# Window attention into a SiLU MLP: another order of the work ahead of the MLP, and of the attention beside it

## The chip, the core and the metric

The kernel runs on one core of a Trainium2 chip. TensorE (PE in the profile; PEld is its weight loads), VectorE (DVE), ScalarE (ACT) and GpSimd (POOL) each work through their own instructions in order; SyncE (SP) issues most of the DMAs, in order too. The metric is the device time of one launch in microseconds; lower is better. The three timed runs lie within 0.24% of one another.

## The reference

```python
def _attn_ref(q, k, v):                       # (8, 8, 576, 64) each
    scores = scale * np.matmul(q, k.transpose(0, 1, 3, 2))
    bias = slopes[:, None, None] * (-np.abs(rel))[None, :, :]
    mask = (rel >= 0) & (rel < 128)
    scores = np.where(mask, scores + bias[None], -1000000000.0)
    scores = scores - np.max(scores, axis=-1, keepdims=True)
    attn = np.exp(scores)
    attn = attn / (np.sum(attn, axis=-1, keepdims=True) + 1e-09)
    return np.matmul(attn, v)
...
x = attn_out.transpose(0, 2, 1, 3).reshape(4608, 512)
h = x @ w_in                                  # 512 x 2048
g = h * (1.0 / (1.0 + np.exp(-h)))
return g @ w_out                              # 2048 x 512
```

A query looks at itself and the 127 positions before it. The attention's output, with the heads side by side, is the input of a SiLU MLP.

## The kernel before

**Attention in pairs.** The 4608 tokens are 36 tiles of 128. Two batches of 576 tokens make nine tiles, and tile `i` needs the keys and values of tiles `i - 1` and `i`. Its eight heads are done in two halves of four, so there are 72 "pairs" `p = 2i + q`. A pair goes through these steps: `scores` (16 matmuls into the PSUM tiles `sp`; 8 in the first tile of two batches), `row_max` (four DVE instructions that add the bias from `tab` and take the maximum), `exps` (four ACT instructions), `p_hi` and `p_lo` (ACT and DVE: the probabilities as an fp16 high and low part, tile `hr`, two buffers), `p_transpose` (two DMA transposes issued by SP, into `hl`), `attend` (24 matmuls into `av`, with V's two parts `v1`, `v2`), `normalize` (DVE: sum, reciprocal, product), and for tiles from the fifth on `x_hi` and `x_lo` (ACT and DVE). Tiles 0 to 3 leave their output as fp32 `x` instead, and `x_transpose` (PE, then ACT and DVE) makes the MLP's first input `xh`, `xl` of it, one chunk of 128 columns at a time. Later tiles go through a DMA transpose and `x_parts` (ACT and POOL).

**V's scale.** `v_hi` (POOL) and `v_lo` (DVE) need one power of two for each two batches of V. `vscale_load` brings V in nine pieces of 256 KB, `vscale_reduce` reduces each to one column (an ACT instruction), and `vscale_finish` makes the scale `vsc` of them in three stages on DVE and PE. For the first two batches no `attend` can run before it.

**The MLP in groups.** A group is four tiles, 512 tokens; there are nine. For each of 16 slices `f` of the inner width, `gemm1` (`h`, 12 matmuls in two halves), `act1` (tanh, ACT), `act2` (DVE), `act3` (`gh`, ACT), `act4` (`gl`, POOL) and `gemm2` (`o`, 12 matmuls in two halves). Both matrices are kept as a high and a low part in SBUF, made once from the fp64 weights: `w_load`, then `w_split1`, `w_hi` (ACT), `w_shift`, `w_low`, `w_sign` (DVE), `w_lo` (DVE for `wil`, POOL for `wol`). Four of the 32 halves are made ahead of the MLP (`W_EARLY`), 28 beside its first group. The raw halves have two buffers.

**What sets the order.** Nothing is scheduled by a tool: the engines run what the program records, in that order. The program counts points; a group's 64 half-slices are points 0 to 63 of it (1 point is about 6 matmuls of the MLP), and negative points precede the MLP. `put(point, fn, ...)` plans a step, and `begin()` records a point's steps ahead of that point's matmuls. `at(p)` is the point of `scores(p)`; the pair's other steps have fixed distances to it. `later(n, ...)` puts a step `n` points on, behind what is planned there already. A group's last slice is special: `gemm2` of slices 14 and 15 follow each other, with `x_parts` of the next group's tiles between the halves, and `store` sends the group's output (two `ot` on ACT, two on DVE, with two buffers for all).

**PSUM.** During the MLP, `scores` takes both buffers of the bank `a`, `attend` takes one, and both wait for DVE to have read what was in them.

Of the kernel before, what the change touches and what calls it, by code (L numbers as in the profile page):

```python
# [6 lines left out]
F32 = mybir.dt.float32  # L7
# [24 lines left out]
GT = TG // P  # L32
NF = DFF // P
NCC = DM // P
# [5 lines left out]
VCH = 9  # L40
# [5 lines left out]

SLICE = 4
STEP = 8
LEAD = 26
XD = GT  # L50
LAST = [f"{kind}{f}" for f in (NF - 1, NF - 2) for kind in ("wih", "wil", "woh", "wol")]
WD = (1, 1, 1, 2, 3)
W_EARLY = (-52, -40, -28, -14)


def at(p):

    return STEP * (p - 2 * GT) - LEAD


@with_exitstack
def tile_window_attention_then_silu_mlp(ctx, tc, qk, v, w_in, w_out, base8, out):
    nc = tc.nc

    const = ctx.enter_context(tc.tile_pool(name="const", bufs=1))
# [32 lines left out]
    bank = {"scores": [("w", "x"), ("y", "z")], "av": ["a"], "misc": ["h"]}  # L98
    turn = {}
# [10 lines left out]
    vred = {}  # L110

    def vscale_load(b, i):
        tag, bufs = (LAST[4 + i % 4], 1) if b == 0 else ("rv", 2)
        t = pool.tile([P, DM], F32, tag=tag, bufs=bufs, name=f"vm{b}_{i}")
        (nc.scalar if b == 0 else nc.sync).dma_start(t, v[b, i * P : (i + 1) * P, :])
        vred.setdefault(b, {})[i] = t

    def vscale_reduce(b, i):
        t = vred[b][i]
        if i == 0:  # L120
            vred[b]["m"] = pool.tile([P, VCH], F32, tag="vm", name=f"vmx{b}")
        m = vred[b]["m"][:, i : i + 1]

        nc.scalar.activation(t, t, AF.Abs, accum_out=m)

    def vscale_finish(b, stage):
        r = vred[b]
# [138 lines left out]
    xt, whole, now = {}, [], [0]  # L266
# [40 lines left out]
    def x_transpose(cc):  # L307
        xp = ps_of(next_tag("misc"), f"xp{cc}")
        for i in range(GT):
            nc.tensor.transpose(xp[:, i * P : (i + 1) * P], xt[i][:, cc * P : (cc + 1) * P], ident)  # L310
        nc.scalar.copy(xh[:, cc], xp)  # L311
        nc.vector.tensor_sub(xl[:, cc], xp, f32(xh[:, cc]))  # L312
# [132 lines left out]
    def put(point, fn, *a):  # L445
        plan.setdefault(max(point, at(0)), []).append((fn, a))

    for p in range(NPAIR):
        i, q = divmod(p, 2)
        n = at(p)  # L450
        put(n, scores, p)
        if block_of(i) in (SPLIT, SPLIT + 1):
            put(n + 1, other_batch, p)
        put(n + 1, row_max, p, 0)
        put(n + 2, row_max, p, 1)
        put(n + 2, exps, p, 0)
# [12 lines left out]
        if q == 0:  # L469
            if i > 1:  # L470
                put(n - 14, load_q, i)
                put(n - 14, load_k, i)
            put(n - 2, load_v, i)
            put(n + 9, v_hi, i)
            put(n + 10, v_lo, i)
    for b in range(1, NBB):
        n = at(2 * NBLK * b)
        for i in range(VCH):
# [36 lines left out]
            fn(*a)  # L515

    with tc.manual_schedule():
        load_q(0)
        load_k(0)
        nc.scalar.dma_start(tab, base8)  # L520
        load_q(1)
        load_k(1)
        for i in range(4):
            vscale_load(0, i)
        make_identity(nc, ident)
        nc.gpsimd.memset(v1[:, :, :, D : D + 1], 1.0)
        nc.gpsimd.memset(ones, 1.0)
        for i in range(VCH):
            put(at(0) + 1 + i // 2, vscale_reduce, 0, i)
            if i + 4 < VCH:  # L530
                put(at(0) + 1 + i // 2, vscale_load, 0, i + 4)
        for x in range(3):
            put(at(0) + 6 + x, vscale_finish, 0, x)
        for n in range(2):
            put(at(0) + 4 + n, w_next_load)
        for n in W_EARLY:
            put(n, w_next)
        while pos[0] < 0:
            begin()
            pos[0] += 1  # L540
        bank.update(scores=[("a", "a")], misc=["a"])
        for cc in range(NCC - 1):
            turn["misc"] = -1
            bank["misc"] = ["h"]
            x_transpose(cc)
        bank["misc"] = ["a"]

        for g in range(NG):
            now[0] = g

            seq = []
            for f in range(NF):
                n = g * NF + f
                seq += [("g1", n, 0)] + [("xt", 0, NCC - 1)] * (n == 0) + [("g1", n, 1)]
                if 0 < f < NF - 1:
                    seq += [("g2", n - 1, 0), ("g2", n - 1, 1)]
            n = g * NF + NF - 1
            for i, x in enumerate([("g2", n - 1, 0), ("g2", n - 1, 1), ("g2", n, 0), ("g2", n, 1)]):
                if g + 1 < NG:
                    seq.append(("xt", g + 1, i))  # L560
                seq.append(x)
            for k, n, half in seq:
                if k == "xt":
                    if n == 0:
                        bank["misc"] = ["h"]
                        x_transpose(half)
                        bank["misc"] = ["a"]
# [58 lines left out]
```

## Time and profile before

| | |
|---|---|
| median of 3 runs | 1053.81 us (1052.30 to 1054.81) |
| the profiled execution | 1053.94 us, of which the span from the first to the last instruction is 1052.2 us |
| PE busy | 965.3 us, 92% of the span |
| DVE busy | 525.2 us, 50% |
| ACT busy | 464.8 us, 44% |
| POOL busy | 256.3 us, 24% |
| DMA | 109.62 MB, mean 104 GB/s |

Shares over the whole span hide that there are three stages: what precedes the MLP, the MLP's first group (with the weights made beside it), and the eight other groups. They are told apart by busy times in stretches of the span. Rows of the timeline give the start, the duration and, in brackets, the idle time of the engine just before with what ended it.

### The profile page before, as it was taken

Reading aid. Unit: us, or ns where it says so; the run is one execution under the profiler, and the core shown is the slowest. Engines: PE = TensorE matmul, PEld = TensorE weight load, DVE = VectorE, ACT = ScalarE, POOL = GpSimd, SP = SyncE. Lnnn points to the kernel's source line nnn. Section 1 sums busy time; section 2 is a strip of 40 time slices with the busy share of each in tenths; the row PEclk is TensorE's granted clock in tenths of the full one; section 3 lists DMA queues with packets and bytes.
Section 4 is the critical chain, followed back from the end, with each engine's and each line's share of the span. In section 5 each row is a group of like instructions: output and inputs, shape, how many; then the busy total and the mean of one; then the engine's idle time right before and its main releaser. Section 6 shows DMA issues by size and latency. Waiting matters only on the chain. (4 is left out here: it accounts for less than half of the span.)

```text
span 1052.2 us, 16631 instructions
## 1 busy us (share of the span) xinstructions
PE 965.3 (92%) x6204; PEld 773.6 (74%) x6204; DVE 525.2 (50%) x1374; ACT 464.8 (44%) x975; POOL 256.3 (24%) x236
## 2 busy tenths in 40 slices
PE   3557787799999999999999999999999999999998
PEld 2445666678887888788878887878788878887886
DVE  2777999944444544434445444434445444421111
ACT  5555656544445444534454445434534453423222
POOL 0011333332223222322232222222222232222221
PEclk9768999999999999999999999999999999999999
DMA  7885677644444444424454445423444443311001
GB/s 218 172 196 156 199 193 208 174 118 89 82 91 116 106 103 100 104 70 82 88 117 101 102 102 121 89 72 82 110 75 90 84 110 82 63 22 41 1 0 40
DMA packets 214560, 109.62 MB, mean 104 GB/s; under 512 B 181072, under 2 KB 189264, under 8 KB 214480
## 3 DMA queue, kind: packets, MB, share of 16 engines
q1 hardware_dynamic: 213040, 105.68, 43.1%
q10 hardware_dynamic: 1440, 2.88, 0.8%
q8 instruction: 49, 0.80, 0.3%
q14 instruction: 31, 0.25, 0.1%
HBM read 55.05 MB, written 9.44 MB: 61 GB/s over the span
## 5 line engine op out<-in xcount | busy, mean ns | idle before, releaser
L367 POOL TENSOR_TENSOR gl<-gt,gh 128x512 fp32r<-128x512 f32 x144 | 187.7, 1303 | 637.5 <-ACT gh L362 428.6
L351 ACT ACTIVATE gt<-h 128x512 f32<-128x512 f32 x144 | 85.6, 595 | 424.0 <-PE h L344 424.0
L344 PE MATMUL h<-xh,wih 128*128 128x512 f32 x576 | 237.6, 413 | 0.0
L379 PE MATMUL o<-woh,gl 128*128 128x512 f32 x576 | 226.0, 392 | 7.0 <-POOL gl L367 6.9
L344 PE MATMUL h<-xh,wil 128*128 128x512 f32 x576 | 226.4, 393 | 0.0
L344 PE MATMUL h<-xl,wih 128*128 128x512 f32 x576 | 226.0, 392 | 0.2 <-DVE xl L312 0.2
L379 PE MATMUL o<-woh,gh 128*128 128x512 f32 x576 | 225.4, 391 | 0.2 <-ACT gh L362 0.2
L379 PE MATMUL o<-wol,gh 128*128 128x512 f32 x576 | 224.3, 389 | 0.0
L356 DVE SCALAR_TENSOR_TENSOR gt<-gt,h 128x512 f32<-128x512 f32 x144 | 98.8, 686 | 249.2 <-ACT gt L351 249.1
L238 DVE SCALAR_TENSOR_TENSOR hr<-t,hr 128x512 f16<-128x512 f32 (+1 forms) x144 | 131.3, 912 | 91.8 <-ACT hr L233 91.1
L214 DVE CUSTOM_DVE_ANT_0 t<-sp,tab 128x256 f32<-128x256 f32 (+1 forms) x288 | 103.2, 403 | 80.3 <-PE sp L194 80.3
L379 PEld LDWEIGHTS o<-woh,gl 128*128 128x128 f32 x576 | 108.1, 188 | 36.6 <-POOL gl L367 14.3
L224 ACT ACTIVATE t<-t,mx 128x256 f32<-128x256 f32 (+1 forms) x288 | 121.2, 487 | 27.3 <-DVE mx L214 26.5
L344 PEld LDWEIGHTS h<-xh,wih 128*128 128x128 f32 x576 | 109.0, 189 | 25.7 <-ACT xh L311 0.4
L344 PEld LDWEIGHTS h<-xh,wil 128*128 128x128 f32 x576 | 108.8, 189 | 24.0
L379 PEld LDWEIGHTS o<-woh,gh 128*128 128x128 f32 x576 | 108.1, 188 | 22.8 <-ACT gh L362 0.5
L379 PEld LDWEIGHTS o<-wol,gh 128*128 128x128 f32 x576 | 108.1, 188 | 22.2
L344 PEld LDWEIGHTS h<-xl,wih 128*128 128x128 f32 x576 | 109.2, 190 | 19.9 <-DVE xl L312 0.5
L194 PE MATMUL sp<-k,q 64*128 64x128 f32 x1088 | 93.0, 309 | 23.0 <-DMA k<-qk 6.5
L194 PEld LDWEIGHTS sp<-k,q 64*128 64x128 f32 x1088 | 76.9, 207 | 46.8 <-issue 44.9
L362 ACT CAST gh<-gt 128x512 fp32r<-128x512 f32 x144 | 88.6, 615 | 33.3 <-DVE gt L356 33.3
L261 PEld LDWEIGHTS <-hl 128*128 128x128 f16 x1632 | 57.5, 101 | 51.6 <-issue 36.9
(52 smaller groups left out, 609.6 us busy)
## 6 DMA issues: line engine op xcount, KB each, us to landing
q<-qk SPq DMA_DIRECT2D x36, 256.0 KB, 3.5
k<-qk SPq DMA_DIRECT2D x36, 256.0 KB, 3.5
rv<-v SPq DMA_DIRECT2D x36, 256.0 KB, 3.0
out<-ot SPq DMA_DIRECT2D x36, 256.0 KB, 2.0
wr<-w_in SPq DMA_DIRECT2D x16, 512.0 KB, 4.0
wr<-w_out SPq DMA_DIRECT2D x16, 512.0 KB, 3.7
vm<-v SPq DMA_DIRECT2D x27, 256.0 KB, 3.2
vm<-v ACTq DMA_DIRECT2D x9, 256.0 KB, 3.6
```

The lines of the kernel that those rows point to most:

```text
L194: nc.tensor.matmul(sp[h][:, u, o], qs[i][rows, 2 * q + u], ks[i - 1 + o][rows, 2 * q + u], start=True, stop=True, skip_group_check=True,)
L214: nc.vector.tensor_tensor_reduce(out=t[:, h, 2 * P - n :], in0=st[p]["sp"][h][:, u, o].rearrange("p o c -> p (o c)"), in1=tab[:, 4 * q + 2 ...
L224: nc.scalar.activation(x, x, AF.Exp, bias=st[p]["mx"][:, 2 * u + h : 2 * u + h + 1], scale=-1.0)
L238: nc.vector.scalar_tensor_tensor(out=hr[:, 1], in0=t[:, :, 2 * P - n :], scalar=PSCALE, in1=hr[:, 0], op0=ALU.mult, op1=ALU.subtract)
L261: nc.tensor.matmul(av[:, 2 * u + h, : rhs.shape[-1]], lhs, rhs, start=(n == 0), stop=(n == len(seq) - 1), skip_group_check=True,)
L344: nc.tensor.matmul(hps[n], w[:, cc], x, start=(half == 0 and i == 0), stop=(half == 1 and i == len(seq) - 1), skip_group_check=True,)
L351: nc.scalar.activation(gt, hps[n], AF.Tanh, scale=0.5 / W_SCALE)
L356: nc.vector.scalar_tensor_tensor(out=gt, in0=gt, scalar=1.0, in1=hps[n], op0=ALU.add, op1=ALU.mult)
L362: nc.scalar.copy(gh, gt)
L367: nc.gpsimd.tensor_sub(gl, gt, f32(gh))
L379: nc.tensor.matmul(ops[ti], a[:, t], w, start=(f == 0 and i == 0), stop=(f == NF - 1 and i == len(seq) - 1), skip_group_check=True,)
```

## The change

It changes where steps stand. Pairs 0 to 7 keep a distance of 8 points; pairs 8 to 15 get points of their own (`CLOSE`, 6 apart), of which only pair 8 precedes the MLP; later pairs come 12 points later than before (`LEAD`). `attend` and what follows it get a distance of their own, `a`. The four early weight halves move behind pair 7's scores, and two of the four `x_transpose` now stand inside the first slice of the MLP. V's nine pieces get a buffer each (`LAST` grows from 8 tags to 16) and are loaded at once on SP's queue instead of four and five on ACT's; DVE reduces four of them. The bias table comes in two halves, and K and Q are loaded one tile earlier.

```diff
-LEAD = 26
+LEAD = 14
-LAST = [f"{kind}{f}" for f in (NF - 1, NF - 2) for kind in ("wih", "wil", "woh", "wol")]
+LAST = [f"{kind}{f}" for f in range(NF - 1, NF - 5, -1) for kind in ("wih", "wil", "woh", "wol")]
-W_EARLY = (-52, -40, -28, -14)
+CLOSE = (-4, 2, 8, 14, 20, 26, 32, 38)
+W_EARLY = (-18, -15, -12, -8)
 def at(p):
+    if p < 2 * GT:
+        return STEP * (p - 2 * GT) - 18
+    if p < 4 * GT:
+        return CLOSE[p - 2 * GT]
     return STEP * (p - 2 * GT) - LEAD
...
     def vscale_load(b, i):
-        tag, bufs = (LAST[4 + i % 4], 1) if b == 0 else ("rv", 2)
+        tag, bufs = (LAST[XD + i], 1) if b == 0 else ("rv", 2)
         t = pool.tile([P, DM], F32, tag=tag, bufs=bufs, name=f"vm{b}_{i}")
-        (nc.scalar if b == 0 else nc.sync).dma_start(t, v[b, i * P : (i + 1) * P, :])
+        nc.sync.dma_start(t, v[b, i * P : (i + 1) * P, :])
...
-        nc.scalar.activation(t, t, AF.Abs, accum_out=m)
+        if b == 0 and i % 2:
+            nc.vector.tensor_reduce(m, t, axis=AX.X, op=ALU.max, apply_absolute_value=True)
+        else:
+            nc.scalar.activation(t, t, AF.Abs, accum_out=m)
...
+        a = n + (20 if p < 2 * GT else 15 if p < 4 * GT else 13)
...
-        put(n + 20, attend, p)
-        put(n + 21, normalize, p, 0)
-        put(n + 22, normalize, p, 1)
-        put(n + 23, x_hi, p)
-        put(n + 24, x_lo, p)
+        put(a + 0, attend, p)
+        put(a + 1, normalize, p, 0)
+        put(a + 2, normalize, p, 1)
+        put(a + 3, x_hi, p)
+        put(a + 3, x_lo, p)
         if q == 0:
             if i > 1:
-                put(n - 14, load_q, i)
-                put(n - 14, load_k, i)
-            put(n - 2, load_v, i)
-            put(n + 9, v_hi, i)
-            put(n + 10, v_lo, i)
+                put(at(2 * i - 3) + 1, load_q, i)
+                put(at(2 * i - 3) + 1, load_k, i)
+                put(n - 2, load_v, i)
+            put(a - 3, v_hi, i)
+            put(a - 2, v_lo, i)
...
+        for cc, n in enumerate((23, 24)):
+            put(at(2 * GT - 2) + n, x_transpose, cc)
         while pos[0] < 0:
             begin()
             pos[0] += 1
         bank.update(scores=[("a", "a")], misc=["a"])
-        for cc in range(NCC - 1):
...
-            x_transpose(cc)
...
-                seq += [("g1", n, 0)] + [("xt", 0, NCC - 1)] * (n == 0) + [("g1", n, 1)]
+                seq += [("g1", n, 0)] + [("xt", 0, 2), ("xt", 0, 3)] * (n == 0) + [("g1", n, 1)]
```

How the engines' own orders change at the three places that matter below is shown in rows of the recorded program: line, operation, output<-inputs (a tile's name carries the pair, slice or piece it belongs to, then a buffer number), shape.

SP's queue at the start, before. `q`, `k`, `rv` are a tile's queries, keys and values, `wr` raw weights, `hl` a transposed probability tile; the nine pieces `vm0_*` and the table went through ACT's queue.

```order
L161 DMA q0_129<-qk 128x512
L157 DMA k0_131<-qk 128x512
L161 DMA q1_134<-qk 128x512
L157 DMA k1_136<-qk 128x512
L166 DMA rv0_159<-v 128x512
L246 DMA_TRANSPOSE hl0_0_193<-hr0_0_184 128x4x128
L398 DMA wr0_0_197<-w_in 128x4x256
```

And in the changed kernel, from the eighth of V's nine pieces on (`q0`, `k0`, half of the table and the pieces 0 to 6 stand ahead of these):

```order
L122 DMA vm0_7_147<-v 128x512
L122 DMA vm0_8_149<-v 128x512
L176 DMA rv0_151<-v 128x512
L171 DMA q1_153<-qk 128x512
L167 DMA k1_155<-qk 128x512
L542 DMA tab_65<-base8 128x8x128
L256 DMA_TRANSPOSE hl0_0_184<-hr0_0_176 128x4x128
```

All the loads of the start now share one queue, with `q1`, `k1` and the table's second half behind V's nine pieces.

DVE ahead of the MLP's first `act2`, before. The rows begin at the subtraction for the last transposed chunk of `x`; `wm2_0` is the fifth half of the weights, `hr11_0` belongs to pair 11, `gt0` is that `act2`.

```order
L312 TENSOR_TENSOR xl_126<-xp3_916,xh_125 128x512
L414 TENSOR_SCALAR wm2_0_914<-wm2_0_914 128x512
L419 SCALAR_TENSOR_TENSOR wm2_0_914<-wr2_0_635,wm2_0_914 128x512
L426 SCALAR_TENSOR_TENSOR wm2_0_914<-wr2_0_635,wm2_0_914 128x512
L238 SCALAR_TENSOR_TENSOR hr11_0_925<-t11_0_877,hr11_0_925 128x512
L356 SCALAR_TENSOR_TENSOR gt0_938<-gt0_938,h0_907 128x512
```

In the changed kernel, from pair 7's second `p_lo` on:

```order
L248 SCALAR_TENSOR_TENSOR hr7_1_596<-t7_1_561,hr7_1_596 128x512
L295 TENSOR_TENSOR x2_541<-av5_570,r5_600 128x256
L424 TENSOR_SCALAR wm0_0_607<-wm0_0_607 128x512
L429 SCALAR_TENSOR_TENSOR wm0_0_607<-wr0_0_242,wm0_0_607 128x512
L436 SCALAR_TENSOR_TENSOR wm0_0_607<-wr0_0_242,wm0_0_607 128x512
L186 SCALAR_TENSOR_TENSOR v2_68<-rv3_478,vsc0_226,v1_67 128x512
L450 TENSOR_TENSOR wil0_70<-wm0_0_607,wih0_69 128x512
L424 TENSOR_SCALAR wm0_1_617<-wm0_1_617 128x512
L429 SCALAR_TENSOR_TENSOR wm0_1_617<-wr0_1_295,wm0_1_617 128x512
L436 SCALAR_TENSOR_TENSOR wm0_1_617<-wr0_1_295,wm0_1_617 128x512
```

All five first halves of the weights (`wm0_0` to `wm2_0`) and pair 8 alone now stand between pair 7's last `p_lo` and the first `act2`; pairs 9, 10 and 11 are behind it.

ACT at the end of the third group (slice 47 is its last), before. `gt47` is tanh, `gh47` the high part that `gemm2` waits for; `xh` is `x_parts` of the next group, `vm2_8` a reduction for a later V scale, `x16` an `x_hi`.

```order
L351 ACTIVATE gt47_4371<-h47_4352 128x512
L331 ACTIVATE xh_125<-xt12_3457,vsc1_2047 128x4x128
L124 ACTIVATE vm2_8_4271,vmx2_3264<-vm2_8_4271 128x512
L331 ACTIVATE xh_125<-xt12_3457,vsc1_2047 128x4x128
L295 CAST x16_4387<-xs32_4375 128x256
L362 CAST gh47_4389<-gt47_4371 128x512
```

And in the changed kernel:

```order
L361 ACTIVATE gt47_4291<-h47_4271 128x512
L341 ACTIVATE xh_117<-xt12_3452,vsc1_2225 128x4x128
L234 ACTIVATE t33_0_4278<-t33_0_4278,mx33_4267 128x256 x2
L341 ACTIVATE xh_117<-xt12_3452,vsc1_2225 128x4x128
L234 ACTIVATE t33_1_4296<-t33_1_4296,mx33_4267 128x256 x2
L243 ACTIVATE hr33_0_4313<-t33_0_4278 128x512
L372 CAST gh47_4315<-gt47_4291 128x512
```

Pair 33's four `exps` and a `p_hi` now stand between the last slice's tanh and its `gh`. On PE, the scores that stood between `gemm2` of slices 14 and 15 (pair 35's, in this group) are replaced by pair 33's, one slice earlier, so that nothing stands between these two `gemm2`; and the group's last `attend` stands between the two halves of `gemm2` of slice 15 instead of behind the next group's first `gemm1`.

More of the change, by code (lines that the diff above doesn't have):

```diff
@@ L517, in tile_window_attention_then_silu_mlp @@
     with tc.manual_schedule():
+        make_identity(nc, ident)
+        nc.gpsimd.memset(ones, 1.0)
+        warm = const.tile([P, 1], F32, name="warm")
+        nc.scalar.activation(warm, ones[:, :1], AF.Exp)
         load_q(0)
         load_k(0)
-        nc.scalar.dma_start(tab, base8)
+        nc.sync.dma_start(tab[:, :, P:], base8[:, :, P:])
+        for i in range(VCH):
+            vscale_load(0, i)
+        load_v(0)
         load_q(1)
         load_k(1)
-        for i in range(4):
-            vscale_load(0, i)
-        make_identity(nc, ident)
+        nc.sync.dma_start(tab[:, :, :P], base8[:, :, :P])
         nc.gpsimd.memset(v1[:, :, :, D : D + 1], 1.0)
-        nc.gpsimd.memset(ones, 1.0)
         for i in range(VCH):
-            put(at(0) + 1 + i // 2, vscale_reduce, 0, i)
-            if i + 4 < VCH:
-                put(at(0) + 1 + i // 2, vscale_load, 0, i + 4)
+            put(at(0) + 3 + i // 2, vscale_reduce, 0, i)
         for x in range(3):
-            put(at(0) + 6 + x, vscale_finish, 0, x)
+            put(at(0) + 8 + x, vscale_finish, 0, x)
+        put(at(0) + 12, load_v, 1)
         for n in range(2):
-            put(at(0) + 4 + n, w_next_load)
+            put(at(0) + 14 + 8 * n, w_next_load)
         for n in W_EARLY:
             put(n, w_next)
+        for cc, n in enumerate((23, 24)):
+            put(at(2 * GT - 2) + n, x_transpose, cc)
         while pos[0] < 0:
@@ L564, in tile_window_attention_then_silu_mlp @@
                     if n == 0:
-                        bank["misc"] = ["h"]
                         x_transpose(half)
-                        bank["misc"] = ["a"]
                     else:
```

3 lines of the change are left out of this document (removed).

## The prediction

> **What bounds the kernel now.** First the busy times in the three stages. Columns: stretch, its length, busy us (instructions) of PE, PEld, DVE, ACT, POOL, granted clock, DMA share, GB/s.
>
> ```profile
> 0.00:94.10 94.10, 45.16 (x427) 37.26 (x428) 55.95 (x190) 50.77 (x113) 7.65 (x16) 0.76 0.76 188
> 94.10:209.40 115.30, 94.72 (x584) 73.58 (x584) 110.78 (x212) 68.20 (x139) 40.99 (x30) 1.00 0.70 191
> 209.40:226.60 17.20, 13.71 (x103) 10.77 (x103) 8.48 (x25) 8.84 (x21) 7.22 (x8) 1.00 0.52 128
> 226.60:1052.20 825.60, 811.70 (x5097) 652.01 (x5093) 350.00 (x950) 336.99 (x705) 200.48 (x182) 1.00 0.37 82
> ```
>
> In the last 826 us PE is busy for 812, so each wait added to PE there counts in full, and what DVE or ACT do counts only through such waits. In the MLP's first group DVE is busy for 96% of 115.3 us and PE for 82%: DVE is the bound. Ahead of it no engine reaches 60%: latency, a chain from step to step, is the bound. So the change can gain in the first stretch, can gain or lose DVE work in the second, and can only gain or lose waits in the last.
>
> Then the timeline of the first stretch (start, duration, engine, line, what; in brackets the wait before).
>
> ```profile
> 17.37 0.16 DVE L130 TENSOR_REDUCE vcol<-vmx 128x1 f32<-128x9 f32 x1 [1.89 <-ACT vm L124]
> 19.80 0.16 DVE L146 COPY vsc<-vs 128x2 f32<-128x2 f32 x1 [0.73 <-PE vs L144]
> 26.43 0.69 DVE L238 SCALAR_TENSOR_TENSOR hr<-t,hr 128x512 f16<-128x512 f32 x1 [1.47 <-ACT hr L233]
> 30.01 2.50 PE L194 MATMUL sp<-k,q 64*128 64x128 f32 x16 [2.39 <-DMA q<-qk]
> 32.76 0.69 DVE L238 SCALAR_TENSOR_TENSOR hr<-t,hr 128x512 f16<-128x512 f32 x1 [1.90 <-ACT hr L233]
> 37.49 0.69 DVE L238 SCALAR_TENSOR_TENSOR hr<-t,hr 128x512 f16<-128x512 f32 x1 [1.29 <-ACT hr L233]
> 59.23 0.69 DVE L238 SCALAR_TENSOR_TENSOR hr<-t,hr 128x512 f16<-128x512 f32 x1 [2.13 <-ACT hr L233]
> 94.09 0.68 DVE L356 SCALAR_TENSOR_TENSOR gt<-gt,h 128x512 f32<-128x512 f32 x1
> ```
>
> V's scale is ready at 20.0. The four L238 rows are the first `p_lo` of pairs 2, 3, 4 and 7; the last row is the first `act2`, with which the MLP's first group is in its stride. Pairs 2 to 7 come every 6.56 us on average ((59.23 - 26.43)/5), the fastest 4.73 after the one before.
>
> **The first stretch, term 1.** Up to the scale: 0 to 10 us moved 296 GB/s.
>
> ```profile
> 0.00:10.00 10.00, 1.22 (x8) 0.96 (x8) 0.93 (x8) 3.61 (x8) 0.95 (x8) 1.00 0.84 296
> ```
>
> Now the ninth piece is the 12th load of 0.262 MB: 3.15 MB, 10.6 us at that rate. Its reduction on ACT (0.8 us, an estimate from the 0.6 of ACT's other 128x512 rows, below) and the 2.6 us from `vcol` to `vsc` (17.37 to 19.96) give 14.0 us. `q1`, `k1` and the table's second half are loads 14 to 16, 4.19 MB, 14.2 us: next in line. From `vsc` to pair 2's first `p_lo` it took 6.5 us (19.96 to 26.43), which puts that at 20.6 (before 26.4). The four reductions on DVE have no row of their kind; they lie in DVE's idle time ahead of the scale (0.93 us busy in the first ten), so even at twice the 0.7 us of other 128x512 rows they cost nothing.
>
> Pairs 3 to 7: two things that slowed them leave this stretch, the waits for `q` (2.39 us in the row; K and Q now go out one tile earlier, behind transposes that are waited for anyway) and the early weight halves (2.5 us of DVE each, by the prices below). What stays is the loop `row_max`, `exps`, `p_hi`, `p_lo` over DVE and ACT and the two `hr` buffers, 4.73 at best, 6.56 as it was. I take 5.0, near the fastest, since what made it slower is gone: pair 7 at 45.6.
>
> From there to the first `act2` DVE has 44 instructions; their prices (mean ns after the bar):
>
> ```profile
> L214 DVE CUSTOM_DVE_ANT_0 t<-sp,tab 128x256 f32<-128x256 f32 (+1 forms) x48 | 16.8, 394 | 7.7 <-PE sp L194 7.7
> L238 DVE SCALAR_TENSOR_TENSOR hr<-t,hr 128x512 f16<-128x512 f32 (+1 forms) x23 | 14.7, 641 | 19.8 <-ACT hr L233 19.8
> L176 DVE SCALAR_TENSOR_TENSOR v<-rv,vsc,v 128x512 f16<-128x512 f32 x6 | 4.5, 746 | 1.2 <-POOL v L170 1.2
> L419 DVE SCALAR_TENSOR_TENSOR wm<-wr,wm 128x512 int32<-128x512 int32 x5 | 3.5, 691 | 0.2
> L312 DVE TENSOR_TENSOR xl<-xp,xh 128x512 fp32r<-128x512 f32 x4 | 2.7, 688 | 2.4 <-ACT xh L311 2.4
> L414 DVE TENSOR_SCALAR wm<-wm 128x512 int32<-128x512 int32 x5 | 2.4, 486 | 0.5 <-ACT wm L408 0.5
> L285 DVE TENSOR_TENSOR x<-av,r 128x256 f32<-128x256 f32 x8 | 3.3, 417 | 0.0
> L205 DVE MEMSET sp<- 64x384 f32 x4 | 1.5, 378 | 0.3 <-issue 0.2
> ```
>
> Five weight halves 5 x (0.49 + 2 x 0.69) = 9.3, two `wil` 1.4 and four `xl` 2.8 (0.69 each), four `p_lo` 2.6, pair 8's maxima 4 x 0.39 = 1.6, `v_lo` 0.7, two memsets 0.8, three `normalize` (0.42 and two short ones, some 0.8) 2.4: 21.6 us. Waits: before the first and third `xl` for PE's transposes and ACT (the L312 row: 2.4 in two), for a weight half that is loaded only when DVE has freed its buffer, for `p_lo`: 4.3 in all. So the first `act2` comes at 45.6 + 25.9 = 71.5 instead of 94.1: -22.6. Bounds: 4.73 and 6.56 a pair put it 1.4 lower or 7.8 higher.
>
> **The first group, term 2.** It is bound by DVE, so its DVE instructions count. To point 57, where the last weight half ends, it has one pair more: four maxima, two `p_lo`, a `v_lo` and (tiles 4 and 5 now lie here) two 64x384 memsets and four small ones: 1.6 + 1.3 + 0.7 + 1.4 = +5.0. These prices are those of the first stretch; in the group DVE is slower where POOL runs:
>
> ```profile
> L414 DVE TENSOR_SCALAR wm<-wm 128x512 int32<-128x512 int32 x27 | 17.4, 643 | 2.3 <-ACT wm L408 2.3
> L238 DVE SCALAR_TENSOR_TENSOR hr<-t,hr 128x512 f16<-128x512 f32 x14 | 16.1, 1152 | 0.0
> ```
>
> `p_lo` takes 1152 ns here against 641. POOL's 30 instructions there become 31, so I leave that toll as it is: 27 x 0.16 + 14 x 0.51 = 11.4 us on these two lines; half of it more or less is +-5.7.
>
> **Ends of groups, term 3.** Slice 15's `gh` decides. A slice of before with pair steps between tanh and `gh`, as now stands at each of the first seven groups' ends, and the third group's end:
>
> ```profile
> 634.12 0.39 PE L379 MATMUL o<-woh,gh 128*128 128x512 f32 x1
> 634.38 0.60 ACT L351 ACTIVATE gt<-h 128x512 f32<-128x512 f32 x1 [4.74 <-PE h L344]
> 634.88 1.70 ACT L224 ACTIVATE t<-t,mx 128x256 f32<-128x256 f32 x4
> 637.00 0.61 ACT L362 CAST gh<-gt 128x512 fp32r<-128x512 f32 x1
> 637.68 1.29 POOL L367 TENSOR_TENSOR gl<-gt,gh 128x512 fp32r<-128x512 f32 x1 [6.63 <-ACT gh L362]
> 641.16 0.71 ACT L331 ACTIVATE xh<-xt,vsc 128x512 fp32r<-128x512 f16 x1
> 643.22 1.16 PE L194 MATMUL sp<-k,q 64*128 64x128 f32 x16
> 644.31 0.50 PE L379 MATMUL o<-woh,gh 128*128 128x512 f32 x1
> 645.33 0.50 PE L379 MATMUL o<-woh,gl 128*128 128x512 f32 x1 [0.28 <-POOL gl L367]
> ```
>
> `gh` ended 3.49 us after `gemm2` of the slice before began (634.12 to 637.61). At a group's end two `xh` stand between as well, 0.62 each: 4.73, and `gl` 6.05. PE's cover is that `gemm2`, 2.72 us, without the scores of 1.09 (643.22 to 644.31) that followed it: 2.1 us of wait for `gh` and 0.8 for `gl`, 2.85 with the restart. Before, the third group's end lost 0.45 (645.33 for 644.88), the seven 1.6 together. 7 x 2.85 - 1.6 = +18.3. It can be less only if ACT's order let `gh` pass, which it can't; if `exps` were waited for, more.
>
> **Starts of groups, term 4.** There DVE sat behind an `ot` whose buffer was being stored, and with it a `row_max` that held the bank of the next `attend`, and `act2`. First PE's waits after the first group (us, times, longest), then three of them.
>
> ```profile
> PE av L261 <- DVE mx L214: 6.2, 7, 2.1
> PE o L379 <- POOL gl L367: 5.4, 11, 0.7
> 225.92 0.91 PE L261 MATMUL av<-v,hl 128*128 128x65 f16 x24 [2.08 <-DVE mx L214]
> 651.28 0.88 PE L261 MATMUL av<-v,hl 128*128 128x65 f16 x24 [0.67 <-DVE mx L214]
> 656.04 0.50 PE L379 MATMUL o<-woh,gl 128*128 128x512 f32 x1 [0.58 <-POOL gl L367]
> ```
>
> Now only a `normalize` (0.8 us) stands behind that `ot`, and the next scores come a whole `gemm1` later. By the spacing of the matmuls the waits of `av` cost 2.25 once and 0.83 six times, those of `gl` at starts of groups (six of the eleven) 0.74: -11.7. Late next is that `normalize`, with some 0.3 us to spare; 0 to -11.7 bounds it.
>
> **Clock, term 5, and moved work, term 6.**
>
> ```profile
> 223.20:226.60 3.40, 1.31 (x26) 0.96 (x25) 1.77 (x6) 0.70 (x3) 0.00 (x0) 1.00 0.42 157
> 226.60:230.00 3.40, 3.40 (x15) 2.72 (x12) 2.02 (x6) 1.70 (x4) 1.11 (x1) 0.50 0.20 40
> 124.20:127.60 3.40, 1.91 (x29) 1.75 (x30) 3.33 (x10) 3.03 (x7) 1.28 (x1) 1.00 0.68 220
> ```
>
> After 3.4 us with PE busy for 1.31 the granted clock was 0.50 for the next 3.4 us (15 matmuls in place of some 30: 1.7 us lost); after 1.91 it was not. That drop goes with its wait: -1.7. The new waits, 2.1 and 0.8 us within 3.4, leave as little as 0.5 busy; by where they fall on that grid the drop follows 61% (busy under 1.31) to 96% (under 1.91) of them. I take 75% at 1.6 us: 7 x 0.75 x 1.6 = +8.4; 0 and 11.9 bound it. The Trainium skill's page "TensorE: Matmul & The Clock Gate", section "Part 1: The HAM clock gate", has the clock fall after an idle window of about 3.4 us; by that rule these waits fill none, term 5 would be -1.7 and the sum -11.6. The rows above speak against it: 2.1 us idle sufficed.
>
> Two `scores` of 8 matmuls move from the first group to where PE is the bound: half of 1.09 each, +1.1.
>
> **Sum.** -22.6 + 5.0 + 18.3 - 11.7 + (8.4 - 1.7) + 1.1 = -3.2. Against the profiled execution's 1053.94 us (0.13 above the median) that is 1050.7.
>
> **Rivals.**
> - *The first pairs keep their pace* (the slower side): if transposes landing among loads, not the weights or `q`, held pairs 2 to 7, they stay at 6.56: +7.8, 1058.5. The brackets of the four `p_lo` rows name ACT's `hr`, which waits for just that buffer; against it the 4.73. It is slower than before by over 0.2% from 6.05 a pair on.
> - *The clock holds*: 1050.7 - 8.4 = 1042.3. For it, gaps of 2.4 us in the first group (the 1.91 row) that left the clock at 1.00. The Trainium skill's rule above would give this time too.
> - *No wait at the groups' ends*: without terms 3 and the new drops 1050.7 - 26.7 = 1024.0; only if ACT's rows ran otherwise than they stand.
> - *The first group takes back the front*: POOL's toll on DVE up by half, +5.7: 1056.4.
>
> **Numbers.** Forecast 52% (own range 1046 to 1056: 33 of it faster, 19 the same), first pairs 19% (2 the same), clock 16%, no waits 5%, first group 8% (half the same, half slower). Within 0.2% (2.1 us) is about what a measurement of this kernel cannot tell from no change. Faster 0.54, same 0.25, slower 0.21. The range leaves out 1024.0 and the tails of the others: 1041 to 1059.
>
> **What would show it.** First `act2` near 71 us; pairs 2 to 7 5 us apart; the first group's DVE busy over 95% and some 120 us from `act2` to slice 13; at each of seven group ends a PE wait for `gh` of 2 us and one for `gl` under 1, with clock 0.50 behind most; no waits of `av` at group starts. Wrong it is if the pairs' spacing or the waits at the ends are off: together they are 40 us against a sum of 3.

## The result: 1071.6 us, 1.8% slower, and the profile after

The changed kernel took 1071.64 us (median; 1071.01 to 1072.83) against 1053.69 of the kernel before on the same chip, a ratio of 1.0176 (95% interval 1.0163 to 1.0188). The forecast was 1050.7, at the outside 1059.0. The profiled execution has a span of 1069.2 us, 17.0 more than the 1052.2 of before. Every line number is 10 higher than before, from L124 on.

The stages, cut at the same points of the program as before:

```profile
0.00:75.88 75.88, 34.43 (x339) 28.81 (x341) 47.76 (x153) 38.74 (x85) 7.54 (x14) 0.78 0.78 200
75.88:199.86 123.98, 102.43 (x646) 81.05 (x644) 117.00 (x229) 75.11 (x152) 44.73 (x31) 0.92 0.67 183
199.86:217.10 17.24, 14.86 (x89) 11.19 (x88) 9.29 (x28) 8.63 (x16) 7.20 (x8) 0.90 0.80 187
217.10:1069.20 852.10, 832.75 (x5138) 658.80 (x5136) 404.30 (x970) 342.34 (x716) 204.53 (x183) 0.99 0.35 80
```

The first stretch is 18.2 us shorter, the first group 8.7 longer (123.98 for 115.30), and the last stretch 26.5 longer, of which 21.0 is PE's *busy* time (832.75 for 811.70, with 41 matmuls more). Of these 21.0 some 10 are six drops of the clock, in which a matmul takes longer (a term of the prediction), and some 1 is the moved `scores`; the rest, about 10 us, is what no step of the prediction had. The front, from the timeline of the changed kernel:

```profile
13.76 0.16 DVE L140 TENSOR_REDUCE vcol<-vmx 128x1 f32<-128x9 f32 x1 [0.75 <-ACT vm L134]
16.19 0.16 DVE L156 COPY vsc<-vs 128x2 f32<-128x2 f32 x1 [0.32 <-PE vs L154]
21.53 0.69 DVE L248 SCALAR_TENSOR_TENSOR hr<-t,hr 128x512 f16<-128x512 f32 x1 [1.21 <-ACT hr L243]
27.73 0.69 DVE L248 SCALAR_TENSOR_TENSOR hr<-t,hr 128x512 f16<-128x512 f32 x1 [2.44 <-ACT hr L243]
...
49.22 0.69 DVE L248 SCALAR_TENSOR_TENSOR hr<-t,hr 128x512 f16<-128x512 f32 x1 [1.26 <-ACT hr L243]
...
75.88 0.69 DVE L366 SCALAR_TENSOR_TENSOR gt<-gt,h 128x512 f32<-128x512 f32 x1 [0.23 <-ACT gt L361]
```

The scale is ready at 16.35, pair 2's first `p_lo` comes at 21.53, pair 7's at 49.22, 5.54 us apart on average, and the first `act2` at 75.88. Next PE's waits from 205 to 1000 us (us, times, longest), and the clock at the fourth group's end:

```profile
PE o L389 <- ACT gh L372: 13.0, 7, 1.9
PE o L389 <- POOL gl L377: 4.6, 9, 0.6
```

```profile
535.90:539.30 3.40, 1.05 (x4) 0.30 (x2) 0.71 (x2) 3.27 (x7) 1.19 (x1) 1.00 0.01 2
539.30:542.70 3.40, 3.26 (x29) 2.55 (x29) 1.15 (x2) 1.21 (x2) 1.43 (x3) 0.50 0.61 154
```

The seven waits for `gh` are there and those of `av` at the starts of groups are gone, both as forecast; the clock fell to 0.50 behind each of the seven.

The sixteenth `act2` (slice 15 of the first group) divides the kernel well; its row after the change, then before:

```profile
205.36 0.69 DVE L366 SCALAR_TENSOR_TENSOR gt<-gt,h 128x512 f32<-128x512 f32 x1 [2.01 <-ACT gt L361]
```

```profile
215.13 0.69 DVE L356 SCALAR_TENSOR_TENSOR gt<-gt,h 128x512 f32<-128x512 f32 x1 [0.60 <-ACT gt L351]
```

| | forecast | changed | changed, `warm` of 512 bytes (below) |
|---|---|---|---|
| to the first `act2` (94.09 before) | -22.6 | 75.88: -18.2 | 76.01: -18.1 |
| from there to the sixteenth (121.04) | +5.0 | 129.48: +8.4 | 129.91: +8.9 |
| from there to the end (837.03) | +14.4 | 863.84: +26.8 | 851.1: +14.1 |
| sum | -3.2 | +17.0 | +4.9 |

The forecast of the last row is terms 3 to 6: 18.3 - 11.7 + 8.4 - 1.7 + 1.1.

**Matmuls further apart.** `gemm2` of one slice in the last group, where both kernels do the same; its first and last matmul and the next one, after and then before:

```profile
1003.80 0.39 PE L389 MATMUL o<-woh,gh 128*128 128x512 f32 x1
...
1006.36 0.40 PE L389 MATMUL o<-woh,gl 128*128 128x512 f32 x1
1006.59 0.39 PE L354 MATMUL h<-xh,wih 128*128 128x512 f32 x1
```

```profile
1004.02 0.39 PE L379 MATMUL o<-woh,gh 128*128 128x512 f32 x1
...
1006.51 0.39 PE L379 MATMUL o<-woh,gl 128*128 128x512 f32 x1
1006.74 0.39 PE L344 MATMUL h<-xh,wih 128*128 128x512 f32 x1
```

Twelve matmuls took 2.79 us (233 ns each) after and 2.72 (227) before, with no wait in either. In the changed kernel `gemm2` of slices 0 to 11 and `gemm1` of slices 12 to 15 are so, the rest stay at 227 to 229. The first have one operand among the constants and one in the pool; the others have both in one place. And the change made a tile that neither the description of the change nor its diff above shows: `warm`, 4 bytes a partition, the last of the constants.

```diff
+        warm = const.tile([P, 1], F32, name="warm")
+        nc.scalar.activation(warm, ones[:, :1], AF.Exp)
```

By the addresses in the two programs (no trace holds them) it takes 32 bytes, so everything in the pool (`gh`, `gl`, `hl`, the weights of the last slices) now starts at 224 modulo 256 instead of 192, while the other weights, `xh` and `xl` stay at 192.

### The profile page after: what moved, and what is told of

Same layout as the page of the kernel before. It is cut to its first block, busy times and chain, and to the rows that moved or that the text cites. A ratio compares the mean times of both kernels' runs of the same rounds, so it can differ in the third digit from the quotient of the medians.

```text
span 1069.2 us, 16636 instructions
## 1 busy us (share of the span) xinstructions
PE 984.5 (92%) x6204; PEld 779.8 (73%) x6204; DVE 578.3 (54%) x1378; ACT 464.8 (43%) x968; POOL 264.0 (25%) x236
## 5 line engine op out<-in xcount | busy, mean ns | idle before, releaser
L389 PE MATMUL o<-woh,gh 128*128 128x512 f32 x576 | 233.0, 404 | 13.0 <-ACT gh L372 13.0
L389 PE MATMUL o<-woh,gl 128*128 128x512 f32 x576 | 232.5, 404 | 5.0 <-POOL gl L377 4.9
L389 PE MATMUL o<-wol,gh 128*128 128x512 f32 x576 | 230.3, 400 | 0.0
L248 DVE SCALAR_TENSOR_TENSOR hr<-t,hr 128x512 f16<-128x512 f32 (+1 forms) x144 | 133.6, 929 | 91.6 <-ACT hr L243 91.2
L389 PEld LDWEIGHTS o<-woh,gh 128*128 128x128 f32 x576 | 110.4, 192 | 40.0 <-ACT gh L372 16.1
L389 PEld LDWEIGHTS o<-woh,gl 128*128 128x128 f32 x576 | 110.5, 192 | 36.3 <-POOL gl L377 10.4
L234 ACT ACTIVATE t<-t,mx 128x256 f32<-128x256 f32 (+1 forms) x288 | 120.7, 486 | 20.5 <-DVE mx L224 20.5
L389 PEld LDWEIGHTS o<-wol,gh 128*128 128x128 f32 x576 | 110.4, 192 | 25.2
L271 PE MATMUL av<-v,hl 128*128 128x65 f16 (+1 forms) x1632 | 71.7, 205 | 39.3 <-DVE mx L224 17.8
L271 PEld LDWEIGHTS <-hl 128*128 128x128 f16 x1632 | 62.3, 105 | 60.8 <-issue 54.5
L311 DVE TENSOR_TENSOR x<-xs,x 128x256 f16<-128x256 f32 x64 | 71.0, 1109 | 45.9 <-ACT x L305 44.6
```

The source lines that it names most:

```text
L234: nc.scalar.activation(x, x, AF.Exp, bias=st[p]["mx"][:, 2 * u + h : 2 * u + h + 1], scale=-1.0)
L248: nc.vector.scalar_tensor_tensor(out=hr[:, 1], in0=t[:, :, 2 * P - n :], scalar=PSCALE, in1=hr[:, 0], op0=ALU.mult, op1=ALU.subtract)
L271: nc.tensor.matmul(av[:, 2 * u + h, : rhs.shape[-1]], lhs, rhs, start=(n == 0), stop=(n == len(seq) - 1), skip_group_check=True,)
L311: nc.vector.tensor_sub(xt[i][:, 1, cols], st[p]["x"], xt[i][:, 0, cols])
L389: nc.tensor.matmul(ops[ti], a[:, t], w, start=(f == 0 and i == 0), stop=(f == NF - 1 and i == len(seq) - 1), skip_group_check=True,)
```

## Experiments

**1. `warm` padded to 64 bytes.**

```diff
-        warm = const.tile([P, 1], F32, name="warm")
+        warm = const.tile([P, 16], F32, name="warm")
```

> The changed kernel with one tile made wider: `warm`, 4 bytes a partition that the change added to the constants, becomes 64 bytes, so that everything allocated behind the constants starts 64 bytes after a multiple of 64 again, as before the change, and not 32. Theory A (addresses): a matmul whose stationary and moving operands lie at different offsets within 64 bytes starts its successor 231 to 235 ns later instead of 227; half of the 384 MLP matmuls of each group are of that kind in the changed kernel. The last group, in which the two kernels do the same, is 89.63 us there and 88.28 before: 1.35 us, nine times 12 us. So 1059.5 us (1058 to 1061), all spacings at 227. Theory B (the longer spacings come from transfers or other engines that are busier in the changed kernel): no change, 1071.6.

1073.47 us, 1.0198 (1.0167 to 1.0229); `gemm2` stays at 233 ns. Its four executions took 1070.5, 1070.9, 1076.1 and 1077.0 us; the profiled one is the longest, and two of the clock's drops behind its groups' ends last 6.8 us instead of 3.4. A as stated is wrong: 64 bytes off is no better than 32. By itself this speaks as much for B.

**2. The kernel before with 32 bytes more constants.**

```diff
+    pad = const.tile([P, 1], F32, name="pad")
+    nc.gpsimd.memset(pad, 0.0)
```

> The kernel before the change with one constant of 4 bytes a partition more (written once at the start by POOL, never read), which moves everything allocated behind the constants by 32 bytes; the order of the work is that of before. Theory A (addresses): half of the MLP's matmuls are 231 to 235 ns apart instead of 227, 1053.7 + 9 x 1.35 = 1066 us (1064 to 1067). Theory B (the longer spacings belong to the change's order of work): 1053.7.

1062.46 us, 1.0092 (1.0077 to 1.0107), `gemm2` at 233 ns. So 32 unused bytes cost the untouched kernel 9.5 us; B falls.

**3. and 4. The phase of the late pairs, and `gh` ahead of the pair's steps** (both with the 64-byte `warm`).

```diff
-LEAD = 14
+LEAD = 18
-        a = n + (20 if p < 2 * GT else 15 if p < 4 * GT else 13)
+        a = n + (20 if p < 2 * GT else 15 if p < 4 * GT - 2 else 12)
-        put(a + 3, x_lo, p)
+        put(a + 3 + (p >= 4 * GT), x_lo, p)
```

> The changed kernel with the 64-byte `warm` and, for the pairs from the 16th on, the place of the kernel before on the grid of eight points (scores at 6, attend at 2, x_lo a point after x_hi; 8 points later in the program than before, with two attends of the 14th and 15th pair moved to fit); the start and the first pairs stay as changed. Theory C (the seven ends of groups cost what the trace shows: 7 x (2.03 + 0.79 + 1.7 at half clock) = 31.6 us; the waits of the kernel before in their place cost 1.6 + 11.7 + 1.7 = 15.0): 16.6 less than the 64-byte kernel, 1043 us by theory A. Theory D (a shift of phase only moves waits about): within 4 us of the 64-byte kernel. x_lo on DVE should go from 1.1 us back to 0.42 under either.

1053.9 us, 1.0010 (1.0001 to 1.0020): 19.6 less than run 1's median. Every wait for `gh` is gone. In the profiles it is 29 us shorter than run 1 from the sixteenth `act2` on (839.0 for 868.5), and its first group is 8 longer (138.9 for 130.8): DVE has 3.6 us more work there (124.4 us busy for 120.8) and 4.5 us more idle time, 3.9 of it ahead of `w_shift` for ACT. C holds for the ends (runs 5 and 6 below, which differ in the phase alone, give 20.7 us there for its 16.6); it left out what the first group pays.

```diff
-                        later(1, act2, n)
-                        later(2, act3, n)
-                        later(2, act4, n)
+                        if n % NF == NF - 1:
+                            k = plan.setdefault(pos[0] + 1, [])
+                            k[:0] = [(act2, (n,)), (act3, (n,)), (act4, (n,))]
+                        else:
+                            later(1, act2, n)
...
```

> The changed kernel with the 64-byte `warm` and slice 15's act2, act3 and act4 put ahead of the pair's exps on their engines, one point earlier for act3 and act4; nothing else moves. Theory C (the ends of groups cost 4.5 us each because gh stands behind two exps, an xh and a p_hi on ACT): the wait for gh goes (gh ends 0.5 us before PE asks for it), that for gl falls to some 0.4, the clock stays at 1.00: 7 x 4.1 = 29 us less than the 64-byte kernel, 1031 us by theory A. Theory D (the pair's steps, now later, are waited for in its place: next attend or scores): half of that or less, above 1045.

1064.62 us, 1.0115 (1.0098 to 1.0131): 8.9 less than run 1 where C said 29. PE's waits from 205 to 1000 us, and the clock at the fourth group's end:

```profile
PE sp L204 <- DVE xs L295: 8.2, 6, 2.0
PE av L271 <- DVE v L186: 3.8, 7, 0.5
PE o L389 <- POOL gl L377: 2.6, 9, 0.3
PE sp L204 <- DVE vsc L156: 0.7, 1, 0.7
```

```profile
532.00:535.40 3.40, 2.58 (x14) 1.59 (x13) 1.35 (x4) 3.40 (x9) 3.18 (x4) 1.00 0.01 2
535.40:538.80 3.40, 3.37 (x32) 2.72 (x32) 1.78 (x3) 1.71 (x4) 2.26 (x2) 1.00 0.52 119
```

The wait for `gh` went and no clock drop followed, but 12 us of others took its place: 3.8 for `v_lo`, and 8.2 in which `scores` waited for the `normalize` that stands on DVE behind an `ot`, the one that term 4 named as late next with 0.3 us to spare. That this `ot` waits for a buffer still being stored is inferred: ACT's `ot` of the same end waited 2.59 us for such a store. PE had moved up by more than 0.3 us. D describes it better.

**5. and 6. `warm` of 512 bytes**, in the changed kernel and in version 3.

```diff
-        warm = const.tile([P, 1], F32, name="warm")
+        warm = const.tile([P, 128], F32, name="warm")
```

> The changed kernel with `warm` 512 bytes wide, so that every tile lies at the same offset within 512 bytes as before the change (the 64-byte version left the tiles behind the constants 64 bytes off, and its spacings stayed at 233 ns). Theory A' (the spacing depends on the distance of a matmul's two operands modulo something larger than 64 bytes, at most 512): all spacings back at 226.7 ns, 9 x 1.35 = 12 us less than the changed kernel, 1059.5 us (1058 to 1061). Theory B (the spacings belong to the change's order of work, and the pad in the kernel before acted in another way): 1071.6.

1058.84 us, 1.0053 (1.0034 to 1.0073), all spacings in the last group 227 ns: A' holds, and the kernel is 12.8 us faster than with the `warm` of 4 bytes. The last group in the changed kernel, before, and here:

```profile
973.78:1063.41 89.63, 89.05 (x385) 71.93 (x384) 12.39 (x18) 21.29 (x36) 21.33 (x18) 1.00 0.03 12
```

```profile
957.99:1046.27 88.28, 87.66 (x385) 71.94 (x384) 12.39 (x18) 21.29 (x35) 21.30 (x18) 1.00 0.03 13
```

```profile
963.02:1051.30 88.28, 87.66 (x385) 71.91 (x384) 12.38 (x18) 21.28 (x36) 21.26 (x18) 1.00 0.04 13
```

> The version with the phase of the kernel before for the late pairs (1053.9 with the 64-byte `warm`), with `warm` 512 bytes wide. Theory A': 12 to 13 us less, 1041 us, faster than both kernels. Theory B: 1053.9.

1045.25 us, 0.9922 (0.9900 to 0.9944): faster than both kernels. That is 8.7 us less than version 3, where 12 to 13 was expected. Version 3 has no waits for `gh` and no clock drops behind them; the changed kernel's profile has seven, that of run 5 four. At 1.7 us each those three are 5 of run 5's 12.8 us, and the spacing itself is worth the other 8, the 8.7 here and the 9.5 of run 2. The groups' lengths agree: where both profiles have the drop, run 5's group is 0.6 to 1.0 us shorter than the changed kernel's; where only the changed kernel has it, 2.5 to 2.7. Whether a wait brings a drop depends on where it falls: all drops of an execution start whole multiples of 3.41 us apart, and the waits of one end share a period or are split over two. The period with the waits of the first end in the changed kernel and the next one, then those of the fourth end in run 5:

```profile
208.21:211.62 3.41, 1.77 (x7) 0.99 (x8) 1.45 (x6) 2.60 (x6) 2.37 (x3) 1.00 0.57 159
211.62:215.03 3.41, 3.41 (x30) 3.03 (x30) 1.29 (x2) 1.12 (x3) 0.25 (x1) 0.50 0.74 213
```

```profile
530.30:533.71 3.41, 1.76 (x8) 1.13 (x6) 1.79 (x3) 3.41 (x8) 0.94 (x2) 1.00 0.19 69
533.71:537.12 3.41, 2.56 (x31) 1.77 (x31) 0.99 (x2) 2.52 (x5) 2.62 (x3) 1.00 0.40 77
```

In the changed kernel PE was busy for 1.05 to 1.77 us of these periods at its seven ends, in run 5 for 0.92 to 1.46 at the four ends with a drop and for 1.76, 1.98 and 2.04 at the three without. Version 6's waits from 205 to 1000 us:

```profile
PE o L389 <- POOL gl L377: 4.9, 10, 0.6
PE av L271 <- DVE mx L224: 2.9, 2, 2.6
```

**7. and 8. 128 and 256 bytes in the kernel before** (the edit of 2 with other widths).

> The kernel before with a constant of 128 bytes a partition more; the order of work as before. If operands 128 bytes apart (modulo 512) count as aligned, all MLP spacings are 226.7 ns and the time 1053.0; if not, the spacings of gemm2 are 233 ns as with 32 bytes and the time some 1062.

> The kernel before with a constant of 256 bytes a partition more. If operands 256 bytes apart (modulo 512) count as aligned, all MLP spacings are 226.7 ns and the time 1053.0; if not, the spacings of gemm2 are 233 ns and the time some 1062.

1063.94 us with `gemm2` at 233 ns for 128 bytes; 1053.46 and 227 for 256 (one run each, the kernel before 1053.59). The relation repeats after 256 bytes: 32, 64 and 128 are off it, 256 and 512 on it.

**9. A third `hr` buffer for the first eight pairs** (on 5).

```diff
+    def hr_early(n):
+        return pool.tile([P, 8 * P], F16, tag=LAST[13 + n % 3], bufs=1, name=f"hr{n // 2}_{n % 2}")
...
+        if p < 2 * GT:
+            hr = hr_first.pop(0) if hr_first else hr_early(2 * p + u)
```

> The changed kernel with the 512-byte `warm` (1058.8) and three hr buffers instead of two for the first eight pairs (in the places of three weights that are written later). Its pairs 2 to 7 came 5.54 us apart where 5.0 was forecast, and ACT waited 4.0 us in that stretch for an hr buffer that a transposing transfer still read. Theory E (the two hr buffers set the pace): 4.8 us apart, pair 7 some 3.6 us earlier, and that much off the time: 1055.2. Theory F (V's loads and v_lo, for which the attends waited 7.9 us, set it, or the first group of the MLP takes the gain back): within 1 us of 1058.8.

1057.22 us, 1.0038 (1.0023 to 1.0053). ACT's waits in that stretch (20 to 48 us), first with two buffers, then with three, and the first `p_lo` of pairs 2 and 7 with three:

```profile
ACT t L234 <- DVE mx L224: 9.4, 8, 1.9
ACT hr L243 <- DMA hl<-hr: 4.0, 4, 2.4
```

```profile
ACT t L234 <- DVE mx L224: 10.5, 8, 2.0
ACT hr L252 <- DMA hl<-hr: 2.2, 1, 2.2
```

```profile
21.18 0.69 DVE L257 SCALAR_TENSOR_TENSOR hr<-t,hr 128x512 f16<-128x512 f32 x1 [1.21 <-ACT hr L252]
...
47.40 0.69 DVE L257 SCALAR_TENSOR_TENSOR hr<-t,hr 128x512 f16<-128x512 f32 x1 [1.26 <-ACT hr L252]
```

Pairs are 5.24 us apart instead of 5.53 (run 5), the first `act2` comes 2.3 us earlier (73.67 for 76.01), and the time is 1.6 less, though its interval overlaps that of run 5: less than half of E. The loop of two buffers is part of the pace; ACT waits longer still for `row_max`.

**10. All nine reductions on ACT** (on 5; the condition for DVE replaced by `False`).

> The changed kernel with the 512-byte `warm` and all nine reductions of V's scale on ACT; the loads stay as changed. Theory G (the pieces land 0.67 us apart and set the scale's time, two engines are not needed): within 0.7 us of 1058.8. Theory H (ACT, 0.72 us a piece beside the first pair's exps and hr of 2.1 us, falls behind): the scale 2.3 us later, at 18.5, and the time 1061.

1058.88 us. G: the scale's column is made at 13.68 us, as with two engines.

```profile
13.68 0.16 DVE L140 TENSOR_REDUCE vcol<-vmx 128x1 f32<-128x9 f32 x1 [3.86 <-ACT vm L134]
```

The second engine adds nothing that shows, so the earlier scale comes with the loads; which part of their new order gives it was not tried.

**11. Pairs 16 to 19 seven points apart** (the 17th to 20th; on 6, and the `attend` of pairs 14 and 15 is back at the changed kernel's distance of 15 points).

```diff
+    if p < 4 * GT + 4:
+        return 50 + 7 * (p - 4 * GT)
```

> The version with the phase of the kernel before for the late pairs and the 512-byte `warm` (1045.25), with the 17th to 20th pair at points 50, 57, 64 and 71, so that the first group has as many pairs as in the changed kernel and the phase is reached in steps of seven. Theory I (the first group is as long as the DVE work that the pairs put in it: 129.9 us from its first act2 to the sixteenth as in the changed kernel, against 138.7): 5.5 us less than 1045.25, 1039.8. Theory K (the phase itself lengthens it): no change, 1045.

1045.08 us, 0.9923 (0.9906 to 0.9939): no gain. To the sixteenth `act2` it took 130.9 us, as I has it, but from there on 838.8 where version 6 took 830.4: a `scores` at 212.3 us waited 4.3 us for `normalize`, and a clock drop of 6.8 us followed, which costs half of that. K has the time, but not its reason: the work left out of the first group was paid at its end.

**12. `v_lo` a point later** (on 5).

```diff
-            put(a - 2, v_lo, i)
+            put(a - (1 if p >= 2 * GT else 2), v_lo, i)
```

> The changed kernel with the 512-byte `warm` and v_lo one point later for the pairs from the ninth on, a point before their attend. In the first group v_lo took 1.48 us four times in place of 0.75, while POOL ran. Theory L (the collision with POOL is one of place): v_lo 0.75 there, 3 us less DVE work in a stretch that DVE bounds, 1056. Theory M (POOL is so busy there that another instruction takes the toll, or the attend waits for v_lo): within 1 us of 1058.8.

1065.48 us, 1.0112 (1.0089 to 1.0134): 6.6 slower than 5. `w_shift` and `v_lo` in the first group, with 5's order and here (count, busy us, mean ns, idle before):

```profile
L424 DVE TENSOR_SCALAR wm<-wm 128x512 int32<-128x512 int32 x27 | 19.9, 738 | 2.1 <-ACT wm L418 2.0
...
L186 DVE SCALAR_TENSOR_TENSOR v<-rv,vsc,v 128x512 f16<-128x512 f32 x4 | 5.9, 1482 | 0.0
```

```profile
L424 DVE TENSOR_SCALAR wm<-wm 128x512 int32<-128x512 int32 x27 | 19.8, 734 | 8.0 <-ACT wm L418 7.9
...
L186 DVE SCALAR_TENSOR_TENSOR v<-rv,vsc,v 128x512 f16<-128x512 f32 x4 | 3.0, 745 | 0.0
```

The mean of 1482 ns is one `v_lo` of 744 and three of 1710 to 1737, each of the three beside POOL. The toll went as L says, and the group still grew from 129.9 to 136.4 us: DVE was busy a little less (119.9 us for 120.5) and idle for 16.5 us instead of 9.4, 7.9 of it ahead of `w_shift` for ACT (2.0 in 5), and an `attend` waited 4.7 for `v_lo` (1.8 in 5). M has the mechanism (an `attend` waits for `v_lo`) but not its size: in this group the order of the steps decides beside DVE's sum.

**13. Only `xh` and `xl` moved, by 128 bytes, in the kernel before** (a pad ahead of them, one behind).

> The kernel before with 128 bytes of padding ahead of xh and xl and 128 behind them: xh and xl alone lie 128 bytes off, everything else at its old offset modulo 256. Theory A'' (the spacing depends on the distance of a matmul's two operands modulo 256): gemm1, whose moving operand is xh or xl, some 233 ns in all 16 slices, gemm2, whose operands lie as before, 226.7; 16 x 12 x 6 ns a group, nine groups: 10 us, 1063. Theory N (each operand's own offset counts, and gl, gh and the weights are what was wrong): gemm1 and gemm2 both 226.7, 1053.

`gemm2` and then `gemm1` of a slice in the last group:

```profile
1001.80 0.39 PE L383 MATMUL o<-woh,gh 128*128 128x512 f32 x1
...
1004.54 0.40 PE L348 MATMUL h<-xh,wih 128*128 128x512 f32 x1
...
1007.33 0.39 PE L383 MATMUL o<-woh,gh 128*128 128x512 f32 x1
```

`gemm1` takes 2.79 us and `gemm2` 2.74, of which the excess over 2.72 is in its first matmuls, behind `gemm1`'s. So it is the relation of a matmul's two operands, not the place of one: the weights that `gemm1` reads lie as before, and in the changed kernel `gemm2` of slices 12 to 15 kept its 227 to 229 ns although `gh`, `gl` and its weights had all moved by 32 bytes. N falls. The one run took 1057.88 us (before 1053.94), less than the 10 us forecast. The last group has the forecast price (from one group's sixteenth `act2` to the next's 89.9 us for 88.6), the seven before it only 0.6 to 0.9 us each. There `gemm1` was slower already: the first six or so of its matmuls behind attention's came 228 to 236 ns apart on average in the kernel before too, so that `gemm1` averaged 229.0 there and 232.2 here.

**14. Versions 6 and 9 together.**

> The version with the phase of the kernel before for the late pairs and the 512-byte `warm` (1045.25), with three hr buffers for the first eight pairs. Theory E' (the third buffer's 1.6 us, measured on the other phase, adds to the phase's gain): 1043.6. Theory F' (the longer first group takes it back): 1045.

1042.64 us, 0.9891 (0.9874 to 0.9907), the fastest version. E' holds: the gains of 9 and 6 add (the first `act2` comes 2.0 us earlier than in 6, 72.35 for 74.35), as far as intervals that overlap (9 with 5, this one with 6) can show it.

## Why the prediction was wrong

**The step that failed** is one that is not in the working at all: the edit that adds `warm` was costed at nothing, without a word. As a tile it moved the pool by 32 bytes against the constants, and half of the MLP's matmuls came 233 ns apart instead of 227. Taking that away gave 1071.64 - 1058.84 = 12.8 us, of which the spacing itself is some 8 and three drops of the clock are 5. Runs 2, 5, 7, 8 and 13 show the effect in both kernels. No rival contained it. The other steps that failed are the terms 1 and 2, 7.8 us too good together.

**Term 1** (-22.6; measured -18.2): 4.4 too much. The scale came at 16.35, not 14.0: the ninth piece was there at 13.0 and not at 10.6 (the row of its reduction, below). The first 10 us moved 236 GB/s where 296 was taken from the kernel before, and by 13.01 us 273 GB/s had moved 3.55 MB, of which the loads up to that piece are 3.15: loads behind it were already under way. Pair 2 was 0.9 late (21.53 for 20.6; the working's own figures, 14.0 + 6.5, give 20.5), the spacing 5.54 instead of 5.0 cost 2.7, and the tail was 26.7 us instead of 25.9. Choosing near the fastest pair was the mis-sized step: what made pairs slow was said to leave this stretch, but 4.0 us of waits for `hr` buffers in transposing transfers stayed (shown with run 9). The first rival had named them; its 6.56 was 1.0 too slow, the 5.0 chosen 0.5 too fast.

```profile
13.01 0.63 ACT L134 ACTIVATE vm<-vm 128x512 f32<-128x512 f32 x1 [0.64 <-DMA vm<-v]
0.00:10.00 10.00, 2.08 (x16) 1.81 (x16) 2.32 (x11) 4.68 (x12) 0.99 (x8) 1.00 0.75 236
0.00:13.01 13.01, 2.08 (x16) 1.81 (x16) 4.34 (x14) 6.13 (x17) 0.99 (x8) 1.00 0.82 273
```

**Term 2** (+5.0; measured +8.4): 3.4 too little. The stretch from the first to the sixteenth `act2`, before and after:

```profile
94.09:215.13 121.04, 99.17 (x625) 77.40 (x624) 115.28 (x223) 71.34 (x147) 44.41 (x34) 1.00 0.71 191
```

```profile
75.88:205.36 129.48, 107.93 (x680) 85.35 (x678) 120.45 (x242) 76.98 (x156) 48.14 (x35) 0.92 0.69 184
```

DVE's work grew by 5.2 us (115.28 to 120.45), about as forecast, but not by the parts forecast: up to that `act2` there are two pairs more of `row_max`, not one; `v_lo`, priced at 0.7 us, took 0.75 once and 1.74 three times, beside POOL; and the weight halves took 2.9 us less. What the term put at nothing is DVE's idle time, 9.0 us instead of 5.8. Of the 3.3 more, 2.5 stand ahead of `act2`, which waits for tanh on ACT (2.01 ahead of the sixteenth, in its row in the section on the result). So counting DVE's instructions was not enough in this stretch; runs 3 and 12 show the same. Why tanh came later was not taken apart; the granted clock averaged 0.92 here for 1.00 before.

**Terms 3 to 6** (+14.4; measured +14.1 once the operands are back in place). The waits at the seven ends were 2.03 and 0.79 us (read at the fourth), 2.82 against the 2.85 forecast, whose rows near 640 us are of the fifth group's end and not, as the working says, of the third's: the last `act2` of the fifth group starts at 641.3 us there; the waits at the starts went, as forecast; the clock fell behind all seven in the changed kernel and behind four of seven in run 5, against the 75% assumed. The six profiles with these late pairs (the changed kernel, runs 1, 5, 9, 10 and 12) have 30 drops at 42 ends, 71%. That run 5's sum comes so near is in part luck: three more drops would have made it some 5 us more. Run 3 shows that these terms belong to the phase of the pairs on the grid of eight points.

**The rivals.** The clock did not hold and the waits at the ends came. The first pairs kept part of their old pace, 2.7 us of the rival's 7.8, for the reason it gave as far as run 9 shows; 1.7 more came ahead of and behind them. The first group took back 3.4 of 5.7, but not by POOL's toll on DVE: DVE's work grew as forecast. Each had a chance of its own and the forecast neither; together they turn -3.2 into the +4.9 of run 5, slower than before even without `warm`.

## What to carry to other kernels

When a change adds or resizes a tile, work out where everything behind it lands: here a float32r matmul of 128x512 whose two SBUF operands lay 32, 64 or 128 bytes apart modulo 256 took some 3% longer in the last group of every run that had it, with no wait that would show it. So read start-to-start spacings of the same matmul in both traces before looking for waits. And in a kernel bound by one engine, price each periodic step at the points where its period meets the ends of the stages: the place of the late pairs on a grid of eight points was worth 13.6 us (run 6 against run 5), more than the 9.2 that the earlier start kept after the first group had taken its part (18.1 - 8.9).

## What the runs showed of the hardware that was not expected

- In the last group, where no attention runs, float32r matmuls of 128x512 started every 226.7 ns when the operands' offsets were equal modulo 256 bytes and every 233 (231 to 235) when they were 32, 64 or 128 apart. Other distances were not tried. In the groups before it the first six or so matmuls of `gemm1` behind attention's came 228 to 236 ns apart on average at equal offsets too (the kernel before).
- The granted clock fell to 0.50 for 3.4 us after periods in which PE was busy for 1.05 and 1.77 of 3.4 us (changed kernel), and stayed at 1.00 after one with 1.76 (run 5). The Trainium skill's page "TensorE: Matmul & The Clock Gate", section "Part 1: The HAM clock gate", has it fall after an idle window of about 3.4 us; these rows do not agree with it.
- `x_lo` (128x256 on DVE) took 1109 ns on average in the changed kernel, 423 before and 425 in version 6. In the changed kernel 49 of the 64 ran beside POOL's `gl` and averaged 1319 ns, the others 422; in version 6 one did. It is 44 us of DVE's 53 more busy time in the changed kernel, and no row of PE's waits names it.
